# Attention and gated FFN in one kernel: transposes of sequence 1 moved one unit later and into FFN2, V and stores reordered

## The chip, the cores and the metric

The kernel runs on one core of one Trainium2 chip. The metric is device time in microseconds (us) of that core; a median is given with the lowest and the highest run. Every run used here is fast: the granted TensorE clock is between 0.995 and 1.0 in all of them. The profiles quoted are single executions, one for each kernel, and times inside them are counted from the start of the profiled span. The span is some 1.7 us shorter than the device time of the same execution (327.5 us for a run of 329.25 us).

Engines: PE is TensorE's matmuls, PEld its weight loads, DVE is VectorE, ACT ScalarE, POOL GpSimd, SP SyncE. A "q" behind the name is the engine's sequencer.

## The reference, cut to what matters

```python
def _attn_ref(q, k, v):                       # 8 batches, 8 heads, 576 positions, head size 64
    scores = scale * np.matmul(q, k.transpose(0, 1, 3, 2))
    mask = np.abs(pos[:, None] - pos[None, :]) <= 32          # a band
    scores = np.where(mask, scores, -1000000000.0)
    attn = np.exp(scores - np.max(scores, axis=-1, keepdims=True))
    attn = attn / (np.sum(attn, axis=-1, keepdims=True) + 1e-09)
    return np.matmul(attn, v)

def _moe_ref(x, w_gate, w_val, w_out):        # 4608 tokens, 512 wide, 1536 inside
    g = x @ w_gate
    return (g * (1.0 / (1.0 + np.exp(-g))) * (x @ w_val)) @ w_out

def reference(**kwargs):                      # attention, then the FFN on its tokens
    attn_out = _attn_ref(q, k, v)
    x = attn_out.transpose(0, 2, 1, 3).reshape(B * S, H * D)
    return _moe_ref(x, w_gate, w_val, w_out)
```

## The kernel before

The 4608 tokens go in nine chunks of 512. For each chunk the kernel does attention on four tiles of 128 tokens, then FFN1 (12 units, each four gate matmuls, four value matmuls, a Silu on ScalarE and a product hT on VectorE), then FFN2 (hT times the output weights wo). The attention of chunk j+1 is woven into FFN2 of chunk j. Nearly the whole time is dense matmul work (TensorE's matmuls are busy for 97% of the span). The change touches the seams.

K and Q of sequence 1 come as two "long" halves each. (A sequence is one of the 8 batches. Its 576 tokens fill four and a half tiles, so tile 4 is half sequence 0 and half sequence 1.) A half is loaded, cast by VectorE into t, transposed by TensorE in nine matmuls ("turned"), and copied from PSUM into kT or qT by VectorE (640 columns) and ScalarE (512 columns). Before, the four halves are turned behind units 8 to 11 of chunk 0's FFN1:

```python
    load_wo(0, 4)
    load_wo(4, 8)
    load_v(1, (0, 1))
    load_wo(8, FKS)                       # FKS = 12
    load_v(1, (2, 3, 4))
    toks = {}
    for u in range(2, FKS):
        ffn1_unit(0, u)
        nxt = None
        if FKS - 5 <= u < FKS - 1:
            st, *nrest = kq.pop(0)        # K half 1, Q half 1, K half 2, Q half 2
            nxt = cast_long(st, one)      # VectorE
        if u >= FKS - 4:
            turn_long(cast, *rest, turn_tiles((AP_, OP_)), (cp_dve, cp_act))
        if nxt is not None:
            cast, rest = nxt, nrest
```

FFN2 of chunk 0 follows, with the attention of tiles 4 to 7 inside it. A shift is a pair of VectorE copies that moves half of a V block to other partitions; an attention product of an odd block needs it. `s_mask` multiplies the exponentials of a tile by the band on VectorE; `x_dma` sends a normalised tile through a transposing DMA into xT, the input of FFN1.

```python
    def ffn2_first(m):                    # m = 4
        s_group((m, m + 1))               # score products and exp of tiles 4, 5
        s_mask(m)
        shift(1, 1)
        s_mask(m + 1)
        ffn2_part(0, 0, 0, 8)
        ffn2_part(0, 1, 0, 4)
        s_group((m + 2, m + 3))
        ffn2_part(0, 1, 4, 8)
        a_group((m, m + 1))               # attention products and normalisation
        x_dma(m)
        x_dma(m + 1)
        s_mask(m + 2)
        shift(1, 3)
        s_mask(m + 3)
        shift(1, 5)
        ffn2_part(0, 0, 8, FKS)
        ffn2_out(0, 0)
        ffn2_part(0, 1, 8, FKS)
        ffn2_out(0, 1)
        ffn2_part(0, 2, 0, FKS)
        ...                               # next loads
        a_group((m + 2, m + 3))           # tiles 6 and 7
        shift(1, 7)
        ...                               # rest of FFN2, transposes of x
```

Two more places matter. In the head, the second half of Q of sequence 0 is copied behind a V shift:

```python
    turn_mm(qs[1], tiles, True)
    shift_v(0, 3, 4, None, cp_dve)
    turn_out(qT[0], 1, 0, tiles, (cp_dve, cp_act), 0, 11)
```

At the end, the last 128 tokens are written in three pieces, on two queues:

```python
    def ffn2_last(j, sub):
        for c, w, eng in ((0, 256, nc.sync), (256, 128, nc.sync), (384, 128, nc.scalar)):
            ...                           # 12 matmuls of w columns
            cp_act(osb[:, 0:w], ob[:, 0:w])
            eng.dma_start(out=out[r0:r0 + 128, c:c + w], in_=osb[:, 0:w])
```

Of the kernel before, what the change touches and what calls it, by code (L numbers as in the profile page):

```python
# [7 lines left out]
FP32 = mybir.dt.float32  # L8
FP16 = mybir.dt.float16
# [124 lines left out]
def kernel(  # L134
# [10 lines left out]
    nc = tc.nc  # L145
# [8 lines left out]
    NCH = n_tokens // 512  # L154
    FKS = d_ff // 128
# [3 lines left out]
    TP = 9  # L159
# [26 lines left out]
    bandlo = const.tile([128, 64], FP16)  # L186
    iota = const.tile([128, 128], FP16)
    mask = const.tile([128, 4 * HP, 64], FP16)
    warm = const.tile([128, 512], FP16)
    bias = const.tile([128, 2 * HP, 64], BF16)  # L190
    ident_b = const.tile([128, 128], BF16)
    tiny = const.tile([1, 2], FP32)
# [42 lines left out]
        return [pool.tile([128, n, 128], FP16, tag=tag, name="t_ps")  # L235
                for (pool, tag), n in zip(pools, (SC, TP - SC))]

    def turn_mm(t, tiles, cut=False, which=(0, 1)):
        for w in which:
            for j in range(tiles[w].shape[1]):  # L240
                at = SC * w + j
                if cut:
                    for g in range(2):
                        nc.tensor.transpose(
                            out=tiles[w][64 * g:64 * g + 64, j, :],
                            in_=t[:, g, at * D:(at + 1) * D], identity=ident)
                else:
                    nc.tensor.transpose(out=tiles[w][:, j, :],  # L248
                                        in_=t[:, at].rearrange("p g d -> p (g d)"),
                                        identity=ident)  # L250

    def turn_out(dst, x, off, tiles, cps, p0=0, p1=32):
        for at, ps, cp in zip((0, SC), tiles, cps):
            cp(dst[:, :, off + ST * x:off + ST * (x + 1)].rearrange(
                "c e (p j) -> c e p j", j=TP)[:, :, p0:p1, at:at + ps.shape[1]],
               ps.rearrange("c j (p e) -> c e p j", e=HP)[:, :, p0:p1])

    def turn_long(t, dst, x, off, tiles, cps):
        turn_mm(t, tiles)
        turn_out(dst, x, off, tiles, cps)  # L260

    def load_v(b, blocks, gate=None):
        vb = v[b].rearrange("h s d -> s h d")
        for m in blocks:
            lo, hi = max(0, 128 * m - 32), min(S, 128 * m + 96)
            p0 = lo - (128 * m - 32)
            d = nc.gpsimd.dma_start(out=v16[b % 2][p0:p0 + hi - lo, 2 * m, :, 0:D], in_=vb[lo:hi])  # L267
            if gate is not None:
                after(d, gate)

    def shift_v(b, t0, t1, lo, hi):
        vb = v16[b % 2]
        if lo:
            lo(vb[0:64, t0:t1:2], vb[64:128, t0 - 1:t1 - 1:2])
        if hi:
            hi(vb[64:128, t0:t1:2], vb[0:64, t0 + 1:t1 + 1:2])
# [30 lines left out]

    def fill(ps, n):
        for _ in range(n):
            nc.tensor.matmul(out=ps, lhsT=warm[:, 0:128], rhs=warm, start=True, stop=True)  # L310

    xts = {}
    sts = {}
# [44 lines left out]
    def s_mask(m):  # L358
        p = pts[m].rearrange("p g i h q -> p (g i h q)")
        nc.vector.tensor_tensor(out=p, in0=p, in1=mask.rearrange("p a q -> p (a q)"),  # L360
                                op=ALU.mult)
# [52 lines left out]
    def x_dma(m):  # L414
        x16 = x16s.pop(m).rearrange("p a h d -> p (a h d)")
        nc.sync.dma_start_transpose(out=x_out(m), in_=x16)
# [68 lines left out]

    def ffn2_last(j, sub):
        r0 = 512 * j + 128 * sub
        for c, w, eng in ((0, 256, nc.sync), (256, 128, nc.sync), (384, 128, nc.scalar)):
            ob = ps_o.tile([128, 512], FP32, tag="o", name="ob")
            for fk in range(FKS):  # L490
                nc.tensor.matmul(  # L491
                    out=ob[:, 0:w],
                    lhsT=hts[j][:, fk, 128 * sub:128 * sub + 128],
                    rhs=wo16[:, fk, c:c + w],
                    start=(fk == 0), stop=(fk == FKS - 1))
            osb = opool.tile([128, d_model], FP32, tag="osb", name="osb")
            cp_act(osb[:, 0:w], ob[:, 0:w])
            eng.dma_start(out=out[r0:r0 + 128, c:c + w], in_=osb[:, 0:w])

    def check_range():  # L500
        lo = const.tile([128, NPAIR * H], FP32)
# [38 lines left out]

    clean_v(0)
    load_v(0, (0, 1))
    fill(ps_o.tile([128, 512], FP32, tag="o", name="fill"), 10)
    for t in (ident, ident_b):
        nc.vector.tensor_scalar(out=t, in0=iota, scalar1=0.0, scalar2=None, op0=ALU.is_equal)
    nc.vector.tensor_scalar(out=bandlo, in0=iota[:, 0:64], scalar1=0.0, scalar2=None,
# [22 lines left out]
    def shift(b, t):  # L569
        shift_v(b, t, t + 1, cp_dve, cp_dve)  # L570
# [18 lines left out]
    turn_out(kT[0], 1, 32, tiles, (cp_dve, cp_act))  # L589
    tiles = turn_tiles((AP_, OP_))  # L590
    turn_mm(qs[1], tiles, True)
    shift_v(0, 3, 4, None, cp_dve)
    turn_out(qT[0], 1, 0, tiles, (cp_dve, cp_act), 0, 11)
    x_mm(0)
    s_bias(2)
    a_tile(1)
# [30 lines left out]
        kq.append((load_long16(q, 1, x), qT[1], x, 0))  # L627
    load_wo(0, 4)
    load_wo(4, 8)
    load_v(1, (0, 1))  # L630
    load_wo(8, FKS)
    load_v(1, (2, 3, 4))
    toks = {}
    for u in range(2, FKS):
        ffn1_unit(0, u)
        nxt = None
        if FKS - 5 <= u < FKS - 1:
            st, *nrest = kq.pop(0)
            nxt = cast_long(st, one)
        if u >= FKS - 4:  # L640
            turn_long(cast, *rest, turn_tiles((AP_, OP_)), (cp_dve, cp_act))
        if nxt is not None:
            cast, rest = nxt, nrest
# [11 lines left out]
    def s_group(ms):  # L655
        for m in ms:
            s_mm(m)
            s_exp(m)

    def a_group(ms):  # L660
        for m in ms:
            a_mm(m)
            a_norm(m)

    def ffn2_first(m):
        s_group((m, m + 1))
        s_mask(m)
        shift(1, 1)
        s_mask(m + 1)
        ffn2_part(0, 0, 0, 8)  # L670
        ffn2_part(0, 1, 0, 4)
        s_group((m + 2, m + 3))
        ffn2_part(0, 1, 4, 8)
        a_group((m, m + 1))
        x_dma(m)
        x_dma(m + 1)
        s_mask(m + 2)
        shift(1, 3)
        s_mask(m + 3)
        shift(1, 5)  # L680
        ffn2_part(0, 0, 8, FKS)
        ffn2_out(0, 0)
        ffn2_part(0, 1, 8, FKS)
        ffn2_out(0, 1)
        ffn2_part(0, 2, 0, FKS)
        toks[2] = [load_tok(k, 2, ffn2_out(0, 2))]
        a_group((m + 2, m + 3))
        shift(1, 7)
        ffn2_part(0, 3, 0, 6)
        x_pe(m + 2, cp_act, ps_a, "a")  # L690
        ffn2_part(0, 3, 6, FKS)
        ffn2_out(0, 3)
        x_pe(m + 3, cp_dve, ps_a, "a")

    def ffn2(j, m):
        s_group((m, m + 1))
        s_mask(m)
        s_mask(m + 1)
        ffn2_part(j, 0, 0, 6)
        ffn2_part(j, 0, 6, FKS)  # L700
        s_group((m + 2, m + 3))
        a_group((m,))
# [3 lines that stand above are left out]
        ffn2_part(j, 1, 0, 8)  # L706
        ffn2_out(j, 0)
        a_group((m + 1, m + 2, m + 3))
        for i in (1, 2, 3):
            x_dma(m + i)  # L710
        ffn2_part(j, 1, 8, FKS)
        ffn2_out(j, 1)
        for sub in (2, 3):
            ffn2_part(j, sub, 0, 6)
            ffn2_part(j, sub, 6, FKS)
            ffn2_out(j, sub, 2 if (j, sub) == (NCH - 2, 3) else 1)

    ffn2_first(4)
    for j in range(1, NCH):
# [53 lines left out]
```

## Time and profile before

| | before |
|---|---|
| device time, median of 4 runs | 329.75 us (329.65 to 329.81) |
| profiled span | 327.5 us |
| first FFN1 product | 16.04 us |
| first FFN1 product of chunk 1 | 53.66 us |
| end of the last matmul | 322.21 us |
| from there to the end of the span | 5.3 us |

The prediction shows the busy shares and the chain up to FFN2. Two more readings of before are needed later. First, the page's row for the score products (line, engine, operation, operands, count, then busy us and mean ns, then idle us of TensorE ahead of them and what ended it):

```profile
L343 PE MATMUL s_ps<-qT,kT 64*128 64x64 f16 x576 | 12.1, 191 | 0.4 <-DVE qT L209 0.2
```

In the whole execution TensorE waits 0.4 us ahead of score products: there is nearly nothing to win at that place. Second, the chain of waits through FFN2 of chunk 0 (start us, length us, work):

```profile
44.91 0.71 PE o_ps L377 x32
...
50.05 0.63 PE o_ps L377 x32
...
53.82 0.44 PE g_ps L424 x4
```

The attention products (o_ps) of tiles 4 and 5 stand in one group of 0.71 us, those of tiles 6 and 7 in one of 0.63, and FFN1 of chunk 1 starts at 53.82. (The chain counts a matmul from where the one ahead of it let go, so its times are 0.1 to 0.2 us later than the timeline's 53.66 in the table.)

### The profile page before, as it was taken

The page shows a single profiled execution, that of the slowest core. Times are in us where ns is not written, and L with a number is a line of the kernel's source. Part 1 is how long each engine was busy: PE and PEld are TensorE (multiplying, and loading weights), DVE is VectorE, ACT ScalarE, POOL GpSimd, SP SyncE. Part 2 cuts the span into 40 slices and gives each one's busy share as a digit, 9 for nine tenths or more (in the row PEclk, how much of TensorE's full clock was granted, in tenths as well). Part 3 has the DMA queues.
Part 4 walks back from the last instruction along what each step waited for, and adds up shares of the span by engine and source line. Part 5 has one row for each costly group of instructions (what it writes and reads, how often), then busy time and mean ns, then how long its engine had stood idle before and what let it go on. Part 6 is the DMA issues. An engine that isn't in the chain of part 4 may idle for free.

```text
span 327.5 us, 6891 instructions
## 1 busy us (share of the span) xinstructions
PE 319.2 (97%) x2757; PEld 168.2 (51%) x2759; DVE 160.0 (49%) x316; ACT 152.2 (46%) x218; POOL 104.7 (32%) x136
## 2 busy tenths in 40 slices
PE   8899999999999999999999999999999999999993
PEld 3564646445554455455644564456445644564443
DVE  6754865458245734474346523762367144713420
ACT  4843674337343724372536453544355534643311
POOL 8864605865096007800680049103100000000000
PEclk9999999999999999999999999999999999999999
DMA  9999999999999959995999489939903400150012
GB/s 153 185 199 203 198 132 191 130 152 155 216 124 155 89 126 172 149 111 121 164 130 142 99 165 146 149 85 172 149 10 64 130 0 2 40 155 2 1 64 72
DMA packets 154902, 40.14 MB, mean 123 GB/s; under 512 B 140784, under 2 KB 150640, under 8 KB 154864
## 3 DMA queue, kind: packets, MB, share of 16 engines
q0 software_dynamic: 102640, 18.59, 76.8%
q1 hardware_dynamic: 51936, 20.69, 32.7%
q8 instruction: 23, 0.38, 0.5%
q10 hardware_dynamic: 288, 0.36, 0.4%
q14 instruction: 15, 0.12, 0.2%
HBM read 37.75 MB, written 9.44 MB: 144 GB/s over the span
## 4 chain that ended last, share of the span: by engine, by line
PE 94%; DMA 2%; POOL 2%; DVE 1%; issue 0%; ACT 0%; POOLq 0%; ACTq 0%; DVEq 0%
PE ob L471 29%; PE g_ps L424 28%; PE u_ps L424 28%; PE o_ps L377 3%; PE s_ps L343 3%; DMA v<-in_v_dram 2%; POOL st L213 1%; PE ob L491 1%; PE t_ps L248 1%; POOL v L267 1%; ACT p_t L353 0%; PE xt_ps L404 0%; DVE hT L451 0%; PE s_ps L331 0%; DVE t L209 0%
## 5 line engine op out<-in xcount | busy, mean ns | idle before, releaser
L451 DVE TENSOR_TENSOR hT<-ssb,u_ps 128x512 f16<-128x512 f16 (+1 forms) x110 | 74.5, 678 | 129.6 <-PE u_ps L424 77.5
L424 PE MATMUL u_ps<-xT,wv 128*128 128x512 f16 (+1 forms) x504 | 114.0, 349 | 0.0
L424 PE MATMUL g_ps<-xT,wg 128*128 128x512 f16 (+1 forms) x504 | 113.8, 349 | 0.0
L449 ACT ACTIVATE ssb<-g_ps 128x512 f16<-128x512 f32 (+1 forms) x110 | 64.7, 589 | 100.9 <-PE g_ps L424 100.5
L471 PE MATMUL ob<-wo,hT 128*128 128x512 f16 x420 | 95.5, 380 | 0.0
L424 PEld LDWEIGHTS <-wv 128*128 128x128 f16 x504 | 49.2, 98 | 44.2
L424 PEld LDWEIGHTS <-wg 128*128 128x128 f16 x504 | 49.0, 98 | 43.2 <-DVE xT L209 0.2
L267 POOL DMA_DIRECT2D v<-in_v_dram x40 | 33.9, 869 | 91.9 <-ACT ssb L449 90.1
L471 PEld LDWEIGHTS <-hT 128*128 128x128 f16 x420 | 38.9, 98 | 44.4
L206 ACT ACTIVATE osb<-ob 128x512 f32<-128x512 f32 (+2 forms) x38 | 21.9, 576 | 53.3 <-PE ob L471 51.9
L353 ACT ACTIVATE p_t<-s_ps 128x1024 f16<-128x1024 f32 x36 | 34.9, 1022 | 5.1 <-PE s_ps L343 5.0
L296 POOL DMA_DIRECT2D tok<-in_k_dram x30 | 25.3, 882 | 14.4 <-ACT osb L206 12.7
L296 POOL DMA_DIRECT2D tok<-in_q_dram x30 | 25.5, 857 | 10.5 <-DMA tok<-in_k_dram 6.1
L360 DVE TENSOR_TENSOR p_t<-p_t,mask 128x1024 f16<-128x1024 f16 x32 | 21.4, 688 | 8.8 <-ACT p_t L353 8.8
L389 DVE TENSOR_TENSOR x<-o_ps,rall 128x512 f16<-128x512 f32 x36 | 24.9, 691 | 1.2
L209 DVE COPY v<-v 64x528 f16<-64x528 f16 x60 | 19.0, 316 | 3.6 <-DMA v<-in_v_dram 1.7
L343 PEld LDWEIGHTS <-kT 64*128 64x128 f16 x576 | 9.6, 95 | 8.6 <-issue 7.2
L377 PE MATMUL o_ps<-v,p_t 128*64 128x66 f16 x576 | 13.1, 196 | 0.4 <-ACT p_t L353 0.4
L377 PEld LDWEIGHTS <-p_t 128*64 128x64 f16 x576 | 10.9, 110 | 5.0 <-DVE p_t L360 3.0
L343 PE MATMUL s_ps<-qT,kT 64*128 64x64 f16 x576 | 12.1, 191 | 0.4 <-DVE qT L209 0.2
L449 ACT ACT_TABLE_LOAD x8 | 10.3, 1283 | 0.1
L353 ACT ACT_TABLE_LOAD x8 | 10.3, 1283 | 0.1
(58 smaller groups left out, 85.4 us busy)
## 6 DMA issues: line engine op xcount, KB each, us to landing
out_dram<-osb SPq DMA_DIRECT2D x31, 256.0 KB, 2.3
v<-in_v_dram POOLq DMA_DIRECT2D x24, 128.0 KB, 6.4
tok<-in_k_dram POOLq DMA_DIRECT2D x24, 128.0 KB, 8.4
tok<-in_q_dram POOLq DMA_DIRECT2D x24, 128.0 KB, 9.6
v<-in_v_dram POOLq DMA_DIRECT2D x16, 96.0 KB, 6.1
wo<-in_moe_w_out_dram POOLq DMA_DIRECT2D x3, 512.0 KB, 9.2
st<-in_q_dram POOLq DMA_DIRECT2D x8, 144.0 KB, 5.4
out_dram<-osb SPq DMA_DIRECT2D x9, 128.0 KB, 1.8
```

The source lines that it names most:

```text
L206: return nc.scalar.activation(out=o, in_=i, func=AF.Copy, bias=0.0, scale=1.0)
L267: d = nc.gpsimd.dma_start(out=v16[b % 2][p0:p0 + hi - lo, 2 * m, :, 0:D], in_=vb[lo:hi])
L296: d = nc.gpsimd.dma_start(out=st[0:n, m], in_=sb[128 * m:128 * m + n])
L343: nc.tensor.matmul(out=sts[m][:, g, i, hp, :], lhsT=kT[b % 2][64 * g:64 * g + 64, hp, 64 * t:64 * t + 128], rhs=qT[b % 2][64 * g:64 * g + ...
L353: nc.scalar.activation(out=p.rearrange("p g i h q -> p (g i h q)"), in_=s.rearrange("p g i h q -> p (g i h q)"), func=AF.Exp, bias=0.0, sc ...
L360: nc.vector.tensor_tensor(out=p, in0=p, in1=mask.rearrange("p a q -> p (a q)"), op=ALU.mult)
L377: nc.tensor.matmul(out=o[64 * i:64 * i + 64, h // 4, 66 * (h % 4):66 * (h % 4) + 66], lhsT=p[:, g, i, hp, :], rhs=v16[b % 2][:, t, h, :], ...
L389: nc.vector.tensor_tensor(out=x16, in0=ov[:, :, :, 0:D], in1=r.unsqueeze(3).to_broadcast([128, 2, 4, D]), op=ALU.mult)
L424: nc.tensor.matmul(out=ps[:, at:at + n], lhsT=w[:, g, 128 * fk:128 * fk + 128], rhs=xts[j][:, lo // 128:(lo + n) // 128, g, :], start=(g = ...
L449: a = nc.scalar.activation(out=ssb[:, 0:n], in_=ps[0][:, 0:n], func=AF.Silu, bias=0.0, scale=1.0)
L451: nc.vector.tensor_tensor(out=hts[j][:, fk, lo:lo + n], in0=ssb[:, 0:n], in1=ps[1][:, 0:n], op=ALU.mult)
L471: nc.tensor.matmul(out=obs[sub], lhsT=hts[j][:, fk, 128 * sub:128 * sub + 128], rhs=wo16[:, fk, :], start=(fk == 0), stop=(fk == FKS - 1))
```

## The change

The intent: give the casts and loads of sequence 1 one unit more (turn the halves behind units 9, 10 and 11 and the last one inside FFN2, where it is not needed until tile 6), let the score product of tile 2 in the head pass the V shift that waits for a DMA (until 12.09 us before), load the third part of wo ahead of most of V, and put all the last stores on one queue, ScalarE's.

```diff
     turn_mm(qs[1], tiles, True)
+    turn_out(qT[0], 1, 0, tiles, (cp_dve, cp_act), 0, 11)
     shift_v(0, 3, 4, None, cp_dve)
-    turn_out(qT[0], 1, 0, tiles, (cp_dve, cp_act), 0, 11)
...
     load_wo(4, 8)
-    load_v(1, (0, 1))
+    load_v(1, (0,))
     load_wo(8, FKS)
-    load_v(1, (2, 3, 4))
+    load_v(1, (1, 2, 3, 4))
...
-        if FKS - 5 <= u < FKS - 1:
+        if u >= FKS - 4:
             st, *nrest = kq.pop(0)
             nxt = cast_long(st, one)
-        if u >= FKS - 4:
+        if u >= FKS - 3:
             turn_long(cast, *rest, turn_tiles((AP_, OP_)), (cp_dve, cp_act))
...
     def ffn2_first(m):
         s_group((m, m + 1))
+        tiles = [ps_a.tile([128, TP, 128], FP16, tag="a", name="t_ps")]
+        turn_long(cast, *rest, tiles, (cp_dve,))
         s_mask(m)
-        shift(1, 1)
         s_mask(m + 1)
...
-        a_group((m, m + 1))
+        a_group((m,))
         x_dma(m)
-        x_dma(m + 1)
+        shift(1, 1)
         s_mask(m + 2)
         shift(1, 3)
-        s_mask(m + 3)
-        shift(1, 5)
         ffn2_part(0, 0, 8, FKS)
         ffn2_out(0, 0)
         ffn2_part(0, 1, 8, FKS)
         ffn2_out(0, 1)
+        a_group((m + 1,))
+        x_dma(m + 1)
+        s_mask(m + 3)
+        shift(1, 5)
...
-        for c, w, eng in ((0, 256, nc.sync), (256, 128, nc.sync), (384, 128, nc.scalar)):
+        for c, w in ((0, 256), (256, 128), (384, 128)):
...
-            eng.dma_start(out=out[r0:r0 + 128, c:c + w], in_=osb[:, 0:w])
+            nc.scalar.dma_start(out=out[r0:r0 + 128, c:c + w], in_=osb[:, 0:w])
```

Cut from it: 20 fill matmuls of 256 columns in place of 10 of 512 at the very start, and the output of a few more of the last tiles stored in two pieces.

More of the change, by code (lines that the diff above doesn't have):

```diff
@@ L188 @@
     mask = const.tile([128, 4 * HP, 64], FP16)
-    warm = const.tile([128, 512], FP16)
+    warm = const.tile([128, 256], FP16)
     bias = const.tile([128, 2 * HP, 64], BF16)
@@ L236, in turn_tiles, with turn_mm @@
                 for (pool, tag), n in zip(pools, (SC, TP - SC))]
-    def turn_mm(t, tiles, cut=False, which=(0, 1)):
-        for w in which:
+    def turn_mm(t, tiles, cut=False):
+        for w in range(len(tiles)):
             for j in range(tiles[w].shape[1]):
@@ L309, in fill @@
         for _ in range(n):
-            nc.tensor.matmul(out=ps, lhsT=warm[:, 0:128], rhs=warm, start=True, stop=True)
+            nc.tensor.matmul(out=ps[:, 0:256], lhsT=warm[:, 0:128], rhs=warm, start=True, stop=True)
     xts = {}
@@ L542 @@
     load_v(0, (0, 1))
-    fill(ps_o.tile([128, 512], FP32, tag="o", name="fill"), 10)
+    fill(ps_o.tile([128, 512], FP32, tag="o", name="fill"), 20)
     for t in (ident, ident_b):
@@ L711, in ffn2 @@
         ffn2_part(j, 1, 8, FKS)
-        ffn2_out(j, 1)
+        ffn2_out(j, 1, 2 if j == NCH - 2 else 1)
         for sub in (2, 3):
@@ L715, in ffn2 @@
             ffn2_part(j, sub, 6, FKS)
-            ffn2_out(j, sub, 2 if (j, sub) == (NCH - 2, 3) else 1)
+            ffn2_out(j, sub, 2 if j == NCH - 2 and sub in (2, 3) else 1)
     ffn2_first(4)
```

## The prediction

> **What bounds the kernel now.** I read the page first (shares, then the chain that ended last), then that chain in order of time from 0 to 60 us and from 275 us on, then the timelines of the same stretches.
>
> ```profile
> PE 319.2 (97%) x2757; PEld 168.2 (51%) x2759; DVE 160.0 (49%) x316; ACT 152.2 (46%) x218; POOL 104.7 (32%) x136
> ...
> PE 94%; DMA 2%; POOL 2%; DVE 1%; issue 0%; ACT 0%; POOLq 0%; ACTq 0%; DVEq 0%
> ```
>
> TensorE is 94% of the chain. From 57 us to 311 us the chain is an unbroken row of groups of four 512-column matmuls at 0.86 us, and nothing in the change touches that stretch but the tile numbering. So only three places count: the head (to 16.11 us, first FFN1 product), the passage from FFN1 of chunk 0 to its FFN2 (31 to 54 us), and the tail after the last matmul (322.2 us). Lines of the chain in order of time (start, length, work):
>
> ```profile
> 6.44 5.66 DMA v<-in_v_dram
> 12.09 0.02 issue
> 12.12 0.29 DVE v L209
> 12.41 0.03 issue
> 12.44 0.40 DVE qT L209
> 12.84 0.05 issue
> 12.89 0.41 PE s_ps L343 x16
> ...
> 31.57 0.47 issue
> 32.04 0.47 DVE t L209
> 32.51 0.05 issue
> 32.56 0.68 PE t_ps L248 x9
> ...
> 39.42 0.50 PE t_ps L248 x9
> 39.92 0.34 PE s_ps L343 x16
> 40.26 0.01 issue
> 40.27 0.41 PE s_ps L343 x16
> 40.67 2.70 PE ob L471 x12
> ```
>
> The reader is to see: (1) the first part of Q's second half is copied by VectorE behind a V shift that waits for its DMA until 12.09; (2) VectorE's cast of K's first half waits for its DMA until 32.04, and TensorE resumes at 32.56; (3) after the last FFN1 unit come 0.50 us of transposes, then the score products of tiles 4 and 5 with hardly a pause, then FFN2 at 40.67.
>
> [...]
>
> **The change part by part.**
>
> *Fill.* 10 matmuls of 512 columns become 20 of 256: the same columns, before 4.45 us in all, starting perhaps 0.1 us earlier behind the smaller memset. The first transposes wait for the VectorE cast of K (ends 5.76), which waits for a DMA. Worth 0.
>
> *Q split ahead of shift 3.* VectorE is free from 11.63 and the transposes of Q end at 11.89, so its part is copied by about 12.0. ScalarE's part begins at 11.92 (0.76 us for two) and is ready at about 12.3. In between TensorE has the x transposes and the bias products, to about 12.48[...]. The score product of tile 2 starts there instead of at 12.89: 0.41 us. This does not carry through. Exp of tile 2 needs ScalarE, which copies xT until 13.14 (exp now starts 13.34: 0.2 saved), and exp of tile 3 could then end about 0.5 earlier, at 15.1. But the last attention product in front of FFN1 also needs the four V shifts on GpSimd, whose row in the timeline is 13.42 with 1.98 us, so to 15.40. It starts now at 15.66; it could start at about 15.45. Gain **0.2 us**. The weights do not spoil it: wg's first slab is issued at 8.96 and lands 6.7 us later (15.66, needed at about 15.9), wv's at 9.71 and 7.2 (16.91, needed at about 17.1).
>
> *Transposes one unit later.* K half 1 is cast behind unit 8 and turned behind unit 9. The DMA wait of place (2) goes away. TensorE's stream would have had the transposes at 32.33 (31.47 plus 0.86); they came at 32.56. Gain **0.23 us**. The other casts had their data before: the last long load lands at 30.35 + 5.6 = 35.95.
>
> *Last transposes in FFN2.* This is the part that I think costs. Let T be the moment at which TensorE ends the stream of unit 11 (39.42 before). Before: 0.50 us of transposes and 0.75 of score products, FFN2 from T+1.25. After: K half 2 is turned at T, then the products of tiles 4 and 5, then Q half 2 is turned. In the built program the third product of tile 4 that reads the new K tile waits for VectorE's and ScalarE's copies of **K half 2** (counts 61 and 32), although those products read half 1 only: the recorded dependence covers more than the elements that are read. Before, the same product did not wait for Q half 2's copies, and K half 2 had been copied long since. VectorE's queue in front of that copy is: multiply of unit 11, cast of Q half 2, copy of K half 2. The same three stand one unit earlier in the timeline before:
>
> ```profile
> 37.30 0.69 DVE L451 TENSOR_TENSOR hT<-ssb,u_ps 128x512 f16<-128x512 f16 x1 [0.44 <-PE u_ps L424]
> ...
> 37.90 0.64 DVE L209 COPY t<-st 128x1152 f16<-128x1152 f16 x1
> ...
> 38.46 0.81 DVE L209 COPY kT<-t_ps 128x640 f16<-128x640 f16 x1
> ```
>
> From the multiply's start to the copy's end is 38.46+0.81-37.30 = 1.97 us (1.79 us a unit earlier, 35.07 to 36.86). The multiply starts 0.10 us after T (39.52 against 39.42). So TensorE resumes at T + 0.10 + 1.79 to 1.97 + some 0.05 = T+1.95 to T+2.1. It would have reached that product at T + 0.50 + about 0.2 = T+0.7. Idle: 1.25 to 1.4 us. The old order lost about 0.18 there (0.75 us for two score tiles, 0.57 in the later chunks, as at 277.72), so the new loss is **+1.05 to +1.25, say +1.15**. Then 22 products (about 0.4) and nine transposes (0.5): FFN2 from about T+2.9. The ps_a buffer that Q's turn takes is free by the same copy, so no further wait. T itself comes earlier by one set of transposes, a move and no gain.
>
> *Behind it.* Q half 2 goes in one copy (1.35 us, T+2.9 to T+4.3); its first reader, tile 6, comes at T+2.9+2.6. ScalarE is spared one copy of 0.74, but exp of tile 4 starts at T+2.6 as before (K copy to T+1.28, table load 1.28), against a mask at T+4.3; the attention product of tile 4 follows tiles 6 and 7 and another 0.9 us of FFN2, at about T+7. That holds. Tile 5's attention product moves behind eight FFN2 matmuls (1.7 us), in which VectorE does reciprocal, normalisation and shift 1 (0.21+0.69+0.62): just enough. One more change between short and long products: about 0.1 us, as 12 matmuls in 2.70 against 2.59 show. **+0.1**.
>
> *V(1) block 0 alone.* The third part of wo goes one 128 KB load earlier, about 0.8 us of issue. It was issued at 34.44 and landed 10.6 us later, 45.04, ahead of its use at 45.63: no wait to remove. Block 1 lands where wo did, about 45; its shift comes at about 47. Worth 0 here; it buys slack.
>
> *Last stores.* ScalarE copies at 320.91, 321.63 and 322.30 and now issues between them at about 0.36 to 0.47 us each: the third copy slips about 0.1. The last store before was ScalarE's too (issued 322.61, landing 2.8 us later). **+0.1**, or nothing.
>
> **Sum**: -0.2 - 0.23 + 1.15 + 0.1 + 0.1 = +0.9; I take +0.7, because the tail may gain a little and the change was surely made to gain. 329.79 + 0.7 = 330.5.
>
> **The rivals.**
> - *The change pays as meant: 329.2.* Both head gains arrive (0.43), the wait for K half 2 is short because VectorE's cast runs at 0.45 and TensorE reaches the product late, and one store queue shortens the landing. For it: the two SyncE stores and the ScalarE one land together at the end (64 KB took 3.3 us on SyncE, 2.8 on ScalarE, where 128 KB takes 1.8). Against it: [...]the three operations in front of the wait are measured.
> - *The head gains nothing and the stall is whole: 331.0.* If the exps or GpSimd's shifts slip with VectorE's new order, only 0.23 stands against 1.25. For it: GpSimd's chain is rough in the profile. Against: the weights and the score product are shown waiting for the shift.
> - *A new wait later in FFN2: 331.4 to 331.8.* Shift 1 or shift 5 comes too late for tile 5 or 7, some 0.3 to 0.8 us. For it: VectorE's margin for shift 1 is about 0.2 us. Against: V's blocks land by 47.3 in the trace, and are needed at 47 to 51.
>
> **Range and chances.** Known terms leave about ±0.3 for the stall, ±0.2 for the head, ±0.3 for the tail; together some ±0.5 on one side and a little more towards the rival that pays: 329.3 to 331.3. A change of 2% is 6.6 us; nothing here has that size, for every place touched lies within 60 us and holds less than 2 us of waiting. Same 0.98, either side 0.01.
>
> **What would show it.** Right: the score product of tile 2 at about 12.5; FFN1 from about 15.9; no DMA wait ahead of the first long cast; a TensorE pause of over 1 us in the score products in front of FFN2, put down to the copy of K (kT, on VectorE); FFN2 of chunk 0 from about 41.3 to 41.5; FFN1 of chunk 1 0.6 to 1.1 us later than 53.82, and the difference unchanged to the end. Wrong: scores of tiles 4 and 5 in one run of about 0.8 us, or a later start of FFN2's last parts with a shift as releaser.

The sum: -0.2 - 0.23 + 1.15 + 0.1 + 0.1 comes to +0.92, given as +0.9, and was taken as +0.7. The trace of before shows: four 512-column matmuls 0.86 us, a VectorE copy of 640 elements a partition from PSUM 0.82, the table load 1.28, and 0.94 us of issuing for two stores on SyncE against 0.36 for one on ScalarE. Two figures are estimates. The 1.35 us for Q's half 2 in one copy is in no term of the sum; the copies of before alone, 0.39 us for 220 elements and 0.82 for 640, would give 1.34. The 12.48 is the start of the last bias product in before, 12.27, plus a quarter of the 0.86.

## The result, and the profile after

| | before | after |
|---|---|---|
| device time, median of 4 runs each | 329.75 us (329.65 to 329.81) | 330.46 us (330.29 to 330.82) |
| profiled span | 327.5 us | 328.6 us |
| first FFN1 product | 16.04 | 15.80 |
| first FFN1 product of chunk 1 | 53.66 | 54.96 |
| end of the last matmul | 322.21 | 323.50 |
| from there to the end of the span | 5.3 | 5.1 |

The ratio of the fast runs is 1.0023, with a 95% interval of 1.0006 to 1.0041: within 2%, and slower by a little. Ratios here and below are the mean time of one kernel's fast runs over that of the other's of the same rounds, so they are not quite the ratio of the medians quoted.

The page of the kernel after, its busy shares, the chain's shares, and the row of the score products:

```profile
PE 319.7 (97%) x2767; PEld 169.9 (52%) x2769; DVE 159.3 (48%) x316; ACT 151.5 (46%) x217; POOL 104.5 (32%) x136
...
PE 94%; POOL 2%; DMA 2%; ACT 1%; issue 1%; DVE 0%; ACTq 0%; POOLq 0%; DVEq 0%
...
L343 PE MATMUL s_ps<-qT,kT 64*128 64x64 f16 x576 | 12.1, 191 | 1.4 <-DVE kT L209 1.3
```

The shares look alike; they would not have told anything. The row of the score products does: the same 576 matmuls, but TensorE now waits 1.4 us ahead of them, 1.3 of it for VectorE's copy into kT. The chain of waits shows where:

```profile
12.71 0.34 PE s_ps L343 x16
...
15.86 0.98 PE g_ps L424 x8
...
38.70 0.09 DVE hT L451
38.80 0.51 issue
39.31 0.45 DVE t L209
39.76 0.74 DVE kT L209
40.51 0.14 issue
40.64 0.50 PE s_ps L343 x22
41.14 0.61 PE t_ps L248 x9
41.74 2.59 PE ob L471 x12
```

TensorE ends unit 11 at 38.61, does the nine transposes of K's half 2, and then has only ten score products that it may do (eight of sequence 0 and the first two of sequence 1). Then the chain leaves TensorE and runs through VectorE: the product hT of unit 11, the cast of Q's half 2 (t), the copy of K's half 2 (kT). Only then, at 40.64, do the other 22 score products come. FFN2 starts 3.13 us after the end of unit 11 (41.74 against 38.61); before it was 1.25 us (40.67 against 39.42).

Inside FFN2 of chunk 0, by the same view:

```profile
45.88 0.37 PE o_ps L377 x16
...
48.08 0.37 PE o_ps L377 x16
...
51.15 0.82 PE o_ps L377 x32
...
55.12 0.44 PE g_ps L424 x4
```

The attention products of tiles 4 and 5 now stand apart, and those of tiles 6 and 7 take 0.82 us where they took 0.63: they wait for shift 5, which VectorE does from 50.87 to 51.49. From the start of FFN2 to FFN1 of chunk 1 it is now 13.38 us, before 13.15.

So the difference of 1.30 us at FFN1 of chunk 1 is there, and it stays to the last matmul (322.21 to 323.50). A sum over the places, from the two chains and timelines:

| place | after minus before, us |
|---|---|
| head, read at unit 2 of FFN1 (20.41, then 20.23) | -0.18 |
| unit 2 to the end of unit 11, without the one set of transposes moved (0.50) | -0.13 |
| end of unit 11 to FFN2: 3.13 - 1.25 - 0.50 | +1.38 |
| FFN2 of chunk 0 | +0.23 |
| FFN1 of chunk 1 to the last matmul | 0 |
| last matmul to the end of the span | -0.25 |
| sum | +1.05 |

### The profile page after: what moved, and what is told of

Its sections match the earlier page's. It is cut to its first block, busy times and chain, and to the rows that moved or that the text cites. A ratio compares the mean times of both kernels' runs of the same rounds, so it can differ in the third digit from the quotient of the medians.

```text
span 328.6 us, 6909 instructions
## 1 busy us (share of the span) xinstructions
PE 319.7 (97%) x2767; PEld 169.9 (52%) x2769; DVE 159.3 (48%) x316; ACT 151.5 (46%) x217; POOL 104.5 (32%) x136
## 3 DMA queue, kind: packets, MB, share of 16 engines
HBM read 37.75 MB, written 9.44 MB: 144 GB/s over the span
## 4 chain that ended last, share of the span: by engine, by line
PE 94%; POOL 2%; DMA 2%; ACT 1%; issue 1%; DVE 0%; ACTq 0%; POOLq 0%; DVEq 0%
PE g_ps L424 29%; PE u_ps L424 28%; PE ob L471 28%; PE o_ps L377 3%; PE s_ps L343 3%; DMA st<-in_q_dram 2%; POOL st L213 1%; POOL v L267 1%; PE t_ps L248 1%; PE ob L491 0%; PE xt_ps L404 0%; ACT p_t L353 0%; ACT osb L206 0%; PE s_ps L331 0%; DVE kT L209 0%
## 5 line engine op out<-in xcount | busy, mean ns | idle before, releaser
L209 DVE COPY v<-v 64x528 f16<-64x528 f16 x60 | 18.2, 304 | 2.1 <-DMA v<-in_v_dram 0.3
L388 DVE RECIPROCAL rall<-o_ps 128x8 f32<-128x8 f32 x36 | 7.3, 203 | 7.2 <-PE o_ps L377 6.6
```

## The experiments

Two notes for all of them. The kernels ran in three calls, each on one chip, beside eleven runs of the kernel before: medians of before 329.60 (first call), 329.43 (second), 329.35 us (third). And since the time of one execution varies (the eleven runs of before spread over 1.0, 1.7 and 2.2 us in the three calls), I read the terms from the traces too, as three stretches: the start of the first FFN1 product (the head), from there to FFN1 of chunk 1 (the seam), and from the last matmul to the end of the span (the tail). This is the table, from one profiled execution each:

| kernel | head ends | seam | tail | median us | ratio to before (95%) |
|---|---|---|---|---|---|
| before | 16.04 | 37.62 | 5.34 | 329.75 | |
| after | 15.80 | 39.16 | 5.08 | 330.46 | 1.0023 (1.0006 to 1.0041) |
| after_again | 15.86 | 39.09 | 5.30 | 330.50 | 1.0030 (1.0012 to 1.0048) |
| turns_only | 15.89 | 39.21 | 5.65 | 331.17 | 1.0060 (1.0047 to 1.0074) |
| stores_only | 16.14 | 37.75 | 5.32 | 329.78 | 1.0010 (0.9998 to 1.0023) |
| head_only | 16.13 | 38.54 | 5.23 | 329.74 | 1.0004 (0.9991 to 1.0016) |
| cast_behind | 15.91 | 38.74 | 5.19 | 330.07 | 1.0025 (1.0011 to 1.0040) |
| mend | 16.00 | 38.50 | 5.16 | 329.96 | 1.0018 (1.0000 to 1.0035) |
| mend2 | 16.31 | 38.65 | 5.36 | 330.14 | 1.0021 (1.0004 to 1.0038) |
| pad4 | 15.83 | 37.65 | 5.44 | 329.39 | 1.0005 (0.9986 to 1.0025) |
| one_group | 15.63 | 38.79 | 5.15 | 330.14 | 1.0014 (0.9987 to 1.0041) |
| after_pad | 16.16 | 39.01 | 5.04 | 330.71 | 1.0032 (1.0005 to 1.0058) |
| mend3 | 16.27 | 37.93 | 5.03 | 329.42 | 0.9987 (0.9961 to 1.0013) |

All gave correct results. My theory was that the cost is the stall in front of FFN2 (TensorE waiting behind VectorE's queue for K's half 2). The rivals were that the head, the tail or a later wait in FFN2 make the difference.

### The parts alone: turns_only, stores_only, head_only

The kernel before, with only the unit loop, the order of FFN2 and the V loads changed (shortened and commented here; the removed lines and the order inside FFN2 are as in the change above):

```diff
+        if u >= FKS - 4:          # cast one unit later
+        if u >= FKS - 3:          # turn one unit later
+        turn_long(cast, *rest, tiles, (cp_dve,))     # last half inside FFN2
+    load_v(1, (0,)) ... load_wo(8, FKS) ... load_v(1, (1, 2, 3, 4))
     # head, fill and stores as before
```

> The kernel before with only the moved transposes, the FFN2 passage of chunk 0 and V(1) block 0 (head, fill and stores as before). My theory: all of the loss is in here. TensorE pauses some 1.3 us in the score products of tiles 4 and 5, FFN1 of chunk 1 starts about 1.4 us later than 53.82, and the time is 1.2 to 1.5 us over the kernel before. Rival (the loss is made in the tail or the head): under 0.6 us over.

Measured: 331.17 us against 329.60, ratio 1.0060. The seam is 39.21 us, 1.59 longer than before and the same as in the whole change (39.16 and 39.09). The wait for kT is 1.3 us again. So the loss is all in this part.

The kernel before with only the last stores on ScalarE's queue and the outputs split:

```diff
-        for c, w, eng in ((0, 256, nc.sync), (256, 128, nc.sync), (384, 128, nc.scalar)):
+        for c, w in ((0, 256), (256, 128), (384, 128)):
-            eng.dma_start(...)
+            nc.scalar.dma_start(...)
```

> The kernel before with only the last three stores on ScalarE's queue and the split stores of the last chunk but one. My theory after reading the two traces: SyncE reaches the branch at the end about 1.2 us earlier, its row of closing waits is then bound by the landing of the last store, and the time falls by 0.1 to 0.3 us although ScalarE's last copy slips by about 0.3. The prediction on record expected +0.1 or nothing: the rival.

Measured: 329.78 us, ratio 1.0010 with an interval that holds 1, and a tail of 5.32 us against 5.34. No gain is shown. Over all the traces of the table, the tail is 5.23 to 5.65 us in the four kernels with SyncE's stores (mean 5.42) and 5.03 to 5.36 in the nine with ScalarE's (mean 5.18): if there is a gain, it is some 0.2 us, and the timed runs of this part alone do not show it.

The kernel before with only the two lines of the head exchanged:

```diff
+    turn_out(qT[0], 1, 0, tiles, (cp_dve, cp_act), 0, 11)
     shift_v(0, 3, 4, None, cp_dve)
-    turn_out(qT[0], 1, 0, tiles, (cp_dve, cp_act), 0, 11)
```

> The kernel before with only the two lines exchanged, Q's copies ahead of shift 3. My theory: the first FFN1 product starts about 0.2 us earlier than 16.11 and the time falls by 0.15 to 0.25 us, held there by the exps on ScalarE. Rival: a later wait (weights, K's load) takes it back, then under 0.1 us.

Measured: 329.74 us, ratio 1.0004. The head ended at 16.13, no earlier than before. In its profiled run, which was also its slowest (330.16 us), V landed late, and two lines of the chain of waits tell what bounded the rest:

```profile
7.51 5.98 DMA v<-in_v_dram
...
32.30 10.18 DMA wo<-in_moe_w_out_dram
```

V's load ended at 13.49 (12.09 before), GpSimd's shifts followed, and later FFN2 waited for wo; so the head and the seam of this run say more on loads than on the exchange. But the head ends at 15.83 to 16.14 in the four kernels with the old order (mean 15.98) and at 15.63 to 16.31 in the nine with the new one (mean 16.01). The -0.2 us that the first two profiles show is within this scatter, and the interval of head_only's ratio (0.9991 to 1.0016, some 0.4 us to each side) is wider than it. **No gain in time is shown.**

But the traces show what the scatter of the loads hides, if one counts from the last transpose of Q's second half, which comes right after Q's load. The score product of tile 2 starts 1.22 to 1.25 us after it in the four traces with the old order and 0.91 to 0.92 us in the nine with the new; the exp of tile 3 ends 3.94 to 3.97 and 3.63 to 3.64 us after it. So the exchange does take 0.3 us from that path. In four of the nine (after, after_again, mend2, one_group) the path still ends last, and FFN1 follows it; in the other five GpSimd's last V shift ends 0.07 to 0.41 us after the exp and takes the gain back in part or whole, and in mend3 the first gate weights are late too.

### The queue in front of the copy: cast_behind

If TensorE waits for hT, cast and copy on VectorE, one after the other, then taking the cast (0.45 us) out from in front of the copy must shorten the wait. The changed kernel, with the cast of Q's half 2 behind the copy of K's half 2:

```diff
-        if u >= FKS - 4:
+        if FKS - 4 <= u < FKS - 1:
             st, *nrest = kq.pop(0)
             nxt = cast_long(st, one)
         if u >= FKS - 3:
             turn_long(cast, *rest, turn_tiles((AP_, OP_)), (cp_dve, cp_act))
+        if u == FKS - 1:
+            st, *nrest = kq.pop(0)
+            nxt = cast_long(st, one)
```

> The changed kernel with VectorE's cast of Q half 2 placed behind its copy of K half 2. My theory: the pause in the score products is VectorE's queue in front of that copy, so it falls from 1.29 to about 0.8 us; the cast then ends just when TensorE wants it, and the time falls by 0.4 to 0.5 us against the changed kernel. Rival (the score products wait for ScalarE's copy or for a PSUM buffer): pause and time unchanged.

The chain of waits:

```profile
39.36 0.83 DVE kT L209
...
40.33 0.50 PE s_ps L343 x22
```

The cast has gone from the chain, and the products resume 1.67 us after the end of unit 11 (40.33 - 38.66) instead of 2.03 (40.64 - 38.61). That is 0.36 us, not the cast's whole 0.45, for the two had overlapped: in the change the copy starts 0.37 us after the start of the cast, before the cast has ended. The seam is 38.74, 0.35 to 0.42 shorter. The time is 330.07; its interval overlaps that of the change, so the trace is the evidence here, not the clock on the whole. VectorE's queue is the mechanism.

### The change repeated: after_again

> The changed kernel unaltered, for the same rounds as the next ones. Again 0.6 to 1.0 us over the kernel before, with the pause of 1.3 us in the score products of tiles 4 and 5.

Measured: 330.50 us against 329.43, a ratio of 1.0030. The trace repeats every term of the seam (the products resume at 40.64, FFN2 at 41.74, the last attention product takes 0.82 us). So the cost of the whole change is 0.7 us by one comparison of medians and 1.07 by the other. turns_only cost 1.6 (331.17 - 329.60), and neither of the other parts alone gained anything (the smaller fill was not run apart); the difference of 0.5 to 0.9 us that they seem to give back together is not settled. In the traces the tail holds 0.35 to 0.57 of it (5.65 in turns_only against 5.08 and 5.30).

### Without the stall: mend, mend2

If the stall comes only from the order on VectorE and from a dependence on K's half 2 that the products of tiles 4 and 5 don't need, then both last halves can be turned behind those products, with FFN2 matmuls to cover VectorE:

```diff
     def ffn2_first(m):
         s_group((m, m + 1))
-        tiles = [ps_a.tile([128, TP, 128], FP16, tag="a", name="t_ps")]
-        turn_long(cast, *rest, tiles, (cp_dve,))
+        for sub in (0, 1):
+            ffn2_part(0, sub, 0, 4)
+            tiles = [ps_a.tile([128, TP, 128], FP16, tag="a", name="t_ps")]
+            turn_long(*turns.pop(0), tiles, (cp_dve,))    # K half 2, then Q half 2
         s_mask(m)
         s_mask(m + 1)
-        ffn2_part(0, 0, 0, 8)
-        ffn2_part(0, 1, 0, 4)
+        ffn2_part(0, 0, 4, 8)
         s_group((m + 2, m + 3))
```

> The changed kernel, but K half 2 and Q half 2 are both turned inside FFN2, after the score products of tiles 4 and 5 (which then depend on no copy of a second half), with four FFN2 matmuls ahead of each turn. My theory (the score products wait for the copy of K half 2 only because it stands ahead of them in the program): the pause goes, FFN1 of chunk 1 starts at 53.4 to 53.8 instead of 54.96, and the time falls by 1.1 to 1.5 us against the changed kernel, to about 0.5 under the kernel before. Rival (any turn behind unit 11 costs TensorE a pause, or the second part of wo, landed at 41.4, holds FFN2): under 0.5 us gained.

The chain of waits:

```profile
39.07 0.57 PE s_ps L343 x32
39.64 0.97 PE ob L471 x4
...
42.52 1.37 DVE qT L209
43.89 0.04 issue
43.93 0.53 PE s_ps L343 x24
```

The 32 products of tiles 4 and 5 run in one group of 0.57 us, with K's half 2 not yet turned, and the result is correct. **So those products needed nothing of that half; the 1.3 us were spent on a dependence wider than what is read.** But only 0.59 to 0.66 us of the seam came back (38.50), less than expected. Two new waits took the rest: unit 11 ended at 39.07 instead of 38.61 (0.20 of that is a later head, and 0.25 is TensorE waiting for VectorE's cast ahead of the first long turn), and tile 6 waits 0.36 us for the copy of Q's half 2, the last line but two. Two VectorE copies of 1.36 us each stand behind one another there.

mend2 is the same with shift 5 and mask 7 ahead of the normalisation of tile 5, to take the wait for shift 5 out:

```diff
-        a_group((m + 1,))
-        x_dma(m + 1)
+        a_mm(m + 1)
         s_mask(m + 3)
         shift(1, 5)
+        a_norm(m + 1)
+        x_dma(m + 1)
```

> As mend, with the mask of tile 7 and shift 5 ahead of the normalisation of tile 5 on VectorE. FFN2 of chunk 0 took 13.38 us to the next FFN1 in the changed kernel against 13.05 before; my theory is that some 0.2 of it is tile 7's attention product waiting for shift 5, so another 0.2 us off mend. Rival: xT of tile 5 now arrives too late through the DMA transpose and FFN1 of chunk 1 waits, then slower than mend.

(13.05 us is the timeline's number for before; by the chain it is 13.15.) Measured: 330.14 us, no gain. The attention product of tiles 6 and 7 fell to 0.63 us in the chain, as expected, but FFN1 of chunk 1 then waited, as the summary of waits shows (us in total, times, longest):

```profile
PE g_ps L424 <- ACT osb L206: 0.5, 1, 0.5
```

The normalisation of tile 5, and with it the transfer of its x, had gone behind the shift. The wait was exchanged for another of like size, at another line. The row names ScalarE's copy, which came last by the profile. The trace has the real cause: the transposing DMA of tile 5's x was issued at 51.16 instead of 49.81 in mend and landed at 54.83 instead of 52.21; TensorE's wait record for its semaphore ended at 54.90, and FFN1 began at 54.96. This is the rival that had been named.

### A VectorE record that starts late: pad4 and after_pad

The prediction laid the start of the first long cast at 32.04 to a DMA wait. In the kernel before, the semaphore of that load counts full at 31.52 and VectorE's wait record ends at 31.57; then the cast starts 0.47 us later. In the changed kernel the same 0.47 us stood in front of another operation, the product of unit 8 (its wait record ended at 32.38). Timelines of VectorE, before and after (start us, us, operation, idle ahead of it):

```profile
32.04 0.46 DVE L209 COPY t<-st 128x1152 f16<-128x1152 f16 x1 [0.47 <-DMA st<-in_k_dram]
```

```profile
32.85 0.69 DVE L451 TENSOR_TENSOR hT<-ssb,u_ps 128x512 f16<-128x512 f16 x1 [1.46 <-PE u_ps L424]
```

What the two have in common is their place: each is VectorE's 64th record, semaphore waits counted. To test this, pad4 is the kernel before with four more tiny operations at the head:

```diff
-    nc.vector.memset(tiny, 0.0)
+    for _ in range(5):
+        nc.vector.memset(tiny, 0.0)
```

> The kernel before with four more memsets of two elements at VectorE's head (hidden under its wait for K's load). In every trace so far VectorE's record number 63, counted from 0, starts 0.47 us after its wait ended, whatever it is; in the kernel before it is the cast of K half 1, whose data had landed at 31.52, 0.5 us before the cast's start at 32.04. My theory: it is the number and not the load that delays it, so the cast starts at about 31.6, the transposes at about 32.33 and the delay falls on an earlier multiply, where nothing waits: 0.2 us faster. Rival (the cast waits for its load, as the profile says): cast still at about 32.0, time unchanged.

```profile
29.39 0.69 DVE L451 TENSOR_TENSOR hT<-ssb,u_ps 128x512 f16<-128x512 f16 x1 [1.46 <-PE u_ps L424]
...
112.99 0.69 DVE L389 TENSOR_TENSOR x<-o_ps,rall 128x512 f16<-128x512 f32 x1 [0.23 <-DVE rall L388]
```

The late start moved with the count: record 64 is now the product of an earlier unit (its wait ended at 28.92, so again 0.47 us), and the cast started at 31.69. The first FFN1 product of chunk 1 came at 53.48 instead of 53.66, though the head was earlier by 0.21 too, so the seam gained nothing. Up to the first matmul of FFN2 it had gained 0.11 us (24.46 us from the end of the head instead of 24.57). Then the chain shows FFN2 waiting for the second part of wo, which landed at 41.34, and its fifth matmul came 0.22 us late. And the last matmul ended at 322.21, exactly as before: 0.17 us were lost at 114 us, where the second line shows 0.23 us of idle time ahead of a normalisation that follows at once (0.04 us) in the kernel before. That is record 192, three times 64; it starts 0.40 us after its wait record ended (the same operation in the kernel before: 0.21), here and in the two other padded kernels, and they too have 0.17 to 0.18 us more between FFN1 of chunk 1 and the last matmul. In the kernels without the four operations, record 192 is itself a wait. A delay at every 64th record is not shown: records 128, 256 and 320 are waits in all traces, and record 384, in the padded kernels again such a normalisation, starts after the usual 0.21 us. The time is 329.39, the same.

after_pad is the changed kernel with the same four operations.

> The changed kernel with four two-element memsets more at the head of VectorE's stream, so that its 64th record, which starts 0.47 us after its wait has ended in every trace so far, falls on a product of an earlier unit with slack instead of the product of unit 8, which the turns wait behind. Theory (a hold at a fixed place of the stream): the product of unit 8 starts at about 32.4 instead of 32.85, the first moved transposes at 33.6 instead of 34.04, unit 11 ends 0.3 to 0.45 us earlier (38.15 to 38.3 instead of 38.61), the stall stays 1.3 us and FFN1 of chunk 1 begins 0.3 to 0.45 us earlier (54.5 to 54.65), unless the last part of the output weights (landing 44.55 there) holds FFN2. Time 330.1 or so against 330.5. Rival (the hold belongs to the operation or to the turn, not to the place): the product of unit 8 is held just the same and nothing moves.

Measured: 330.71 us, a miss. The late start moved again, to a product whose wait ended at 29.23, and the first long turn took 0.50 us in the chain instead of 0.60. But the seam gained only 0.08 to 0.15 us (39.01 against 39.16 and 39.09) where I had expected 0.3 to 0.45: VectorE's delay had been mostly hidden behind TensorE's matmuls of unit 9. With the head late in this run (16.16) and 0.17 us lost at record 192, nothing was left. The late start is real and bound to the place, but it is worth 0.1 us in these kernels.

### The order inside FFN2: one_group

The changed kernel, with the attention products of tiles 4 and 5 together and the shifts early, as before:

```diff
-        a_group((m,))
-        x_dma(m)
         shift(1, 1)
+        a_group((m, m + 1))
+        x_dma(m)
+        x_dma(m + 1)
         s_mask(m + 2)
         shift(1, 3)
+        s_mask(m + 3)
+        shift(1, 5)
         ffn2_part(0, 0, 8, FKS)
         ffn2_out(0, 0)
         ffn2_part(0, 1, 8, FKS)
         ffn2_out(0, 1)
-        a_group((m + 1,))
-        x_dma(m + 1)
-        s_mask(m + 3)
-        shift(1, 5)
```

> The changed kernel with the attention products of tiles 4 and 5 in one group again and shifts 1, 3 and 5 and mask 7 ahead of FFN2's third part, as before; everything else as changed. It separates the term 'FFN2 of chunk 0 takes 0.23 to 0.33 us longer' from the stall ahead of it. My theory: those 0.23 to 0.33 us are the attention product of tiles 6 and 7 waiting for shift 5 (0.82 to 0.89 us in place of 0.63) and one more switch between FFN2 and attention. Then the product takes about 0.65 us again, the stall of the score products stays 1.3 us, and the first FFN1 matmul of chunk 1 comes 0.15 to 0.3 us earlier than in the changed kernel (54.7 instead of 54.96). Rival: block 1 of V lands only at 45.5, so shift 1 now stands ahead of the normalisation of tile 4 and the product of tile 5 waits 0.1 to 0.3 us for it; then nothing is gained and the first FFN1 matmul of chunk 1 stays at 54.9 to 55.1. Time 330.0 to 330.5 either way; the trace decides.

```profile
45.77 0.62 PE o_ps L377 x32
...
50.82 0.63 PE o_ps L377 x32
...
54.59 0.44 PE g_ps L424 x4
```

The stall stayed (1.3 us for kT), and FFN2 of chunk 0 took 12.96 us (54.59 - 41.63) instead of 13.38: the two attention groups take 1.25 us together instead of 1.56 in three, and one seam between attention products and FFN2 is saved (0.11). Shift 1 was in time, so the rival is out. The seam is 38.79 and the time 330.14, ratio 1.0014. **Splitting the attention of tiles 4 and 5, with the later shifts that came with it, was a loss of 0.3 to 0.4 us on its own.** (These are single traces; the medians, 330.14 against 330.46 and 330.50, come from different calls.)

### Everything mended: mend3

mend, with the four operations of pad4 and with the score products of tiles 6 and 7 four FFN2 matmuls later:

```diff
         ffn2_part(0, 0, 4, 8)
-        s_group((m + 2, m + 3))
         ffn2_part(0, 1, 4, 8)
+        s_group((m + 2, m + 3))
```

> The mended form (the turns of K's half 2 and Q's half 2 both inside FFN2, behind the score products of tiles 4 and 5) with the four memsets and with the score products of tiles 6 and 7 four FFN2 matmuls later. The mended form gained only 0.45 us of the 1.1 to 1.5 expected; its trace put the rest on the 64th record of VectorE (0.46 us: unit 11 ended 39.07 instead of 38.61) and on tile 6 waiting for the copy of Q's half 2 (0.36 us). If that is so, both go: unit 11 ends at 38.5 to 38.7, tile 6 finds its data there, and FFN1 of chunk 1 begins at 53.6 to 53.9 instead of 54.50; the time is 329.1 to 329.6, that is, as before within 0.3. Rival: another wait takes their place (the mask of tile 6, which now comes about 1 us later, or the last part of the output weights), and FFN1 of chunk 1 stays above 54.2; then 329.8 to 330.1.

Measured: 329.42 us against 329.35, ratio 0.9987 (0.9961 to 1.0013). The seam is 37.93, 1.2 us shorter than in the change and 0.3 longer than before. TensorE waits for no score product any more, and what it waits for in the seam is now a load:

```profile
PE ob L471 <- DMA wo<-in_moe_w_out_dram: 0.4, 1, 0.4
```

In this run the third part of wo landed at 45.60 (44.55 in the change, 45.03 before), as loads were late altogether (the head ended at 16.27). The time is as expected, but FFN1 of chunk 1 began at 54.20, not at 53.6 to 53.9: the wait is one that the rival had named. So the change, with its losses taken out, comes to where the kernel before was, and no form that I ran beats it beyond the scatter.

## Why the prediction was right or wrong

The prediction said 330.5 us (329.3 to 331.3) and within 2%; the median was 330.46, and 330.50 when repeated. The total is right, and its largest term is right in kind and near in size. Several small terms were wrong and cancelled in part. Of its signs, the pause, its cause and the missing DMA wait came as said; FFN2 of chunk 0 came at 41.74 instead of 41.3 to 41.5, and FFN1 of chunk 1 came 1.30 us later in the first trace, outside the 0.6 to 1.1 that had been named.

- **The stall in front of FFN2: right in mechanism, sized too small.** The prediction had TensorE resume 1.95 to 2.1 us after the end of unit 11, from three VectorE operations in order; it resumed after 2.03. cast_behind shortened the wait by taking one of the three away, and mend removed it. The term was +1.15 and came out at +1.38: the 22 products after the pause took 0.50 us, not 0.4, and the nine transposes 0.61, not 0.5.
- **The head, -0.2: the mechanism is there, the gain is not shown in the times.** The score product of tile 2 came at 12.71, not at about 12.5. Counted from Q's transposes it came 0.3 us sooner, and so did the exps, as the prediction had it; where GpSimd's shifts end later, they take this back. In the first trace FFN1 came 0.24 us earlier, which is within the scatter of 13 traces, and head_only's time shows no gain. The second rival, "the head gains nothing and the stall is whole", was right as to the stall; as to the head the times cannot tell.
- **Transposes one unit later, -0.23: right in direction, wrong in cause.** The gain was 0.13 us. The step that failed is "VectorE's cast of K's first half waits for its DMA until 32.04": the load was there at 31.52, and the rest was the late start of record 64, which moved to the product of the next unit instead of going away. pad4 and after_pad show that its place decides.
- **FFN2 behind it, +0.1: too small.** It cost 0.23 us. The extra change between attention products and FFN2 was seen (0.11 in one_group; it is not their length, for behind the nine transposes, short too, FFN2 loses nothing: see the last section); what was missed is that the attention of tiles 6 and 7 now waits for shift 5. The third rival named just this wait, but at 0.3 to 0.8 us. The estimate for Q's half 2 in one copy, 1.35 us, came out at 1.36. The two sizes (0.82 us for 640 elements, 1.36 for 1152) give 1.05 ns an element.
- **V(1) block 0, 0:** no run tested it apart. wo's third part landed 0.48 us earlier in the change, and nothing had waited for it before; in mend3, where FFN2 reaches it earlier, it does become a wait.
- **The last stores, +0.1 or nothing:** the change's trace had a tail 0.25 us shorter. stores_only shows no difference. ScalarE's copies do slip behind its own issues, by more than the 0.1 predicted: the chain of the kernel after has the last copy at 323.87, 1.57 us after that of before (322.30), of which 1.29 is the shift of the whole. Two issues, of 0.36 and 0.34 us, stand between the copies in that chain.

But that slip did not lengthen the tail. In the kernel before, SyncE ends its program at 322.32, shows nothing for 3.0 us, and goes through a row of closing semaphore records from 325.31 on; the last store landed at 325.45, inside that row, and the span ended 2.10 us later. In the kernel after, SyncE ends its program at 322.38, over 1 us ahead of the last matmul, its row is held by the last landing (326.87), and the span ends 1.71 us after it. The trace of stores_only has the same picture: last landing at 326.05, end of the span 1.71 us after it. So SyncE's closing seems to bound the end before and the landing after; this is read from the traces, and the 0.2 us or so that it may be worth cannot be timed. In stores_only another issuing engine made no difference that could be timed (329.78 us against 329.60).

The sum of the prediction's terms, +0.9 taken as +0.7, stands against +1.05 in the traces and +0.71 and +1.07 in the medians. That the number was hit so closely the first time owes something to chance: the stall and FFN2 were undersized by 0.36 together, the transposes gave 0.13 of 0.23, and against that the tail, put at +0.1, was 0.25 us shorter in the first trace.

## What to carry to other kernels

Before you move work out from in front of a consumer, follow the queue of the engine that must finish it: here the copy of K's half 2 went behind a product and a cast on VectorE, and TensorE stood 1.3 us for data that its next products did not read. A recorded dependence can be wider than the elements read, so look in the built program for what an operation waits for, and put the writer of the unneeded half behind the reader. And when the places touched held only a few tenths of waiting before (0.4 us ahead of all score products), moving them about cannot gain more than that, while a new wait can cost several times as much (1.3 us here); compare the terms with the scatter of load landings (0.7 us over the 13 heads here) before believing a gain seen in one trace. A gain smaller than that scatter can still be read from traces, when it is counted from the landing (here 0.3 us in the head, the same in all traces) and not from the start.

## Measured here and left open

- The late start of a VectorE operation at a fixed place in its stream. In all 13 traces the 64th record starts 0.46 to 0.47 us after the wait record ahead of it ended, whatever operation it is; with four operations more it moved to another one, and the 192nd then started 0.40 us after its wait instead of 0.21. What does it is open.
- The end of the span. The 5.03 to 5.65 us from the last matmul to the end of the span also hold the last copy and the last store, which lands 3.24 us after the last matmul before and 3.37 after the change. In both traces SyncE's silence starts as soon as its own program ends: the 3.0 us before began 0.11 us after the last matmul, the 2.7 us after began 1.1 us ahead of it.
- The seams between products of different shape. Here 12 FFN2 matmuls (on 128 by 128 of the array) take 2.70 us behind score products (64 by 128; 40.67 in before) or attention products (128 by 64; 48.46 in after) and 2.59 behind the nine transposes (128 by 128; 41.74 in after), so 0.11 us at each such seam. What causes it was not tested.
